# Which engine waits for the last stores: SyncE or GpSimd

## The chip, the cores and the metric

The kernel runs on one core of a Trainium2 chip. The core has five engines that run their own instruction streams and meet only through semaphores: TensorE (PE, matrix products; its weight loads are listed as PEld), VectorE (DVE), ScalarE (ACT), GpSimd (POOL) and SyncE (SP, which here issues transfers and waits). A transfer (DMA) is issued by SyncE or ScalarE and carried out by sixteen DMA engines; when it has landed, its semaphore has been raised by 16.

The metric is the device time of one execution in microseconds. Timed runs give a median; one more execution is recorded by the hardware profiler, and its instructions, waits and transfers can be asked for. An engine's name with a q behind it (SPq) means its instruction queue: waits and the issuing of transfers are listed there.

## The reference

For 2048 rows `x` of width 512 (all in bf16) the kernel computes a gated sum of two branches:

```python
g = sigmoid((x * gate_w).sum(-1, keepdims=True))
# A: 32 heads of width 16
q, k, v = x @ wqkv
phi(t) = concat(softmax(t @ w_phi), softmax(-(t @ w_phi)))   # per head
o = phi(q) @ (phi(k).T @ v) / (phi(q) @ phi(k).sum(rows) + 1e-6)
a = o @ wo
# B
b = relu(x @ w1) @ w2                                        # inner width 1376
out = g * a + (1 - g) * b
```

## The kernel before, in words

The rows are cut into 16 tiles of 128 (numbered m = 0 to 15) and 4 chunks of 512. All of a tile's work is a list of named tasks; each task has an engine, a function that emits its instructions, and the tasks that it depends on. Per chunk: hidden products `h`, the ReLU into `HT`. Per tile or pair of tiles: key and query projections with `w_phi` folded in, softmax features (ScalarE `ex`, VectorE `mx`, `mn`, `sm`, `rc`, GpSimd `t1`, `t2`, `ra`, `nm`), the sum over rows `kv`. Then per tile: a transposing transfer of the query features (`tq`, SyncE), `nd` (numerator and denominator on TensorE, line 654), `rd` and `o` (VectorE, lines 661 and 663), a second transposing transfer `to` (SyncE, line 668), `b` and `a` (TensorE, lines 676 and 682, accumulating both branches in one PSUM bank), the scaled eviction `oe` (line 730 on ScalarE for tiles 0 to 13, line 733 on VectorE for tile 14), and the store `st` to the output (line 735; ScalarE issues it for tiles 0 to 13, SyncE for tile 14).

The last tile is split by columns into 416 and 96: `b15_0`, `a15_0`, `b15_1`, `a15_1` on TensorE (lines 698 and 709), `oe15_0` on ScalarE (line 716), `oe15_1` on VectorE (line 719), and the stores `st15_0`, issued by ScalarE, and `st15_1`, issued by SyncE (both line 722).

The order of the tasks on each engine is written out by hand in the table `ORDER`; nothing is scheduled when the program is built. `_Graph.number` gives each task a semaphore and a count (each transfer its own semaphore, which reaches 16). `settle` works out which waits each task needs, leaving out those already implied by what its engine knows. `emit` writes the waits and instructions, engine by engine (a task's extra waits appear under line 178).

After all engines have been emitted, one more step follows: `unsettled(e, order)` lists the transfers that engine `e` neither waited for nor can infer to have landed, and drops those that another one of the list implies. The engine then waits for each:

```python
        for t in g.unsettled("sp", order):
            nc.sync.wait_ge(sems[t.sem], t.count)
```

For SyncE that list holds six stores, `st11`, `st12`, `st13`, `st14`, `st15_0` and `st15_1`. In the built program they are three instructions on line 751 that wait for two semaphores each: `st14` and `st13`, `st15_0` and `st12`, `st15_1` and `st11`. They are the last instructions of SyncE. The last GpSimd task is `nm_q8` (line 627), the last ones of ScalarE are `oe15_0` and `st15_0`, of VectorE `oe15_1`, of TensorE `a15_1`. No engine but SyncE waits for these last stores.

Of the kernel before, what the change touches and what calls it, by code (L numbers as in the profile page):

```python
# [182 lines left out]
def bass_gated_mix__linear_kernel_hedgehog__dense_activation_relu__prompt_kernel(  # L183
# [38 lines left out]
    with ExitStack() as es:  # L222
# [52 lines left out]
        g = _Graph()  # L275
# [464 lines left out]
        order = g.schedule()  # L740
        g.number(order)
        g.settle(order)
        sems = {e: nc.alloc_semaphore(f"s_{e}") for e in ENGINES}
# [3 lines left out]
        for e, q in (("sp", nc.sync), ("pool", nc.gpsimd), ("act", nc.scalar), ("dve", nc.vector), ("pe", nc.tensor)):  # L747
            g.emit(e, q, order, sems)

        for t in g.unsettled("sp", order):  # L750
            nc.sync.wait_ge(sems[t.sem], t.count)


# [26 lines left out]
```

## Time and profile before

| | |
|---|---|
| timed runs | 149.95, 150.12, 150.76 us; median 150.12 |
| the profiled execution's own time | 149.87 us |
| its span, from the first to the last of the kernel's instructions | 148.3 us |
| TensorE busy | 145.5 us (98%), 1009 matmuls |
| VectorE busy | 111.7 us (75%) |
| GpSimd busy | 109.6 us (74%) |
| ScalarE busy | 91.4 us (62%) |
| granted TensorE clock | 1.000 |
| `out_dram<-OSB` from issue to landing, SyncE: 128 KB, 24 KB | 1.7 us, 1.5 us |
| `out_dram<-OSB` from issue to landing, ScalarE: 128 KB (median of 14), 104 KB | 2.2 us, 1.7 us |

The span covers the kernel's own instructions; the execution's own time is longer, since it takes in what runs around them. Waits, register and branch instructions and the issuing of transfers aren't counted as busy. In the timeline each line gives the start in us from the span's start, the duration in us, the engine, the source line, the operation, what it writes and reads, its shapes and how many were merged; in brackets stands the idle time before it and what ended it. In the view of one source line, three durations (shortest, median, longest, in ns) are followed by the starts of the first and the last instruction. In the view of waits a line gives who waited for whom, the total in us, how often, and the longest.

The trace also keeps a list of every change of a semaphore's value with its time, to the nanosecond, including semaphores that the kernel does not use.

### The profile page before, as it was taken

Reading aid. Unit: us, or ns where it says so; the run is one execution under the profiler, and the core shown is the slowest. Engines: PE = TensorE matmul, PEld = TensorE weight load, DVE = VectorE, ACT = ScalarE, POOL = GpSimd, SP = SyncE. Lnnn points to the kernel's source line nnn. Section 1 sums busy time; section 2 is a strip of 40 time slices with the busy share of each in tenths; the row PEclk is TensorE's granted clock in tenths of the full one; section 3 lists DMA queues with packets and bytes.
Section 4 is the critical chain, followed back from the end, with each engine's and each line's share of the span. In section 5 each row is a group of like instructions: output and inputs, shape, how many; then the busy total and the mean of one; then the engine's idle time right before and its main releaser. Section 6 shows DMA issues by size and latency. Waiting matters only on the chain.

```text
span 148.3 us, 2542 instructions
## 1 busy us (share of the span) xinstructions
PE 145.5 (98%) x1009; PEld 75.3 (51%) x1009; DVE 111.7 (75%) x169; ACT 91.4 (62%) x126; POOL 109.6 (74%) x72
## 2 busy tenths in 40 slices
PE   7999999999999999999999999999999999999994
PEld 2875444445654475445444545455444444445453
DVE  2433666998896948989999997999999988634502
ACT  3475769799969765898983937175583751310141
POOL 4000499999999999999999999999999793150000
PEclk9999999999999999999999999999999999999999
DMA  4998999910040001000000093646957785556752
GB/s 139 324 256 220 169 187 214 340 51 4 0 73 0 0 4 38 0 0 4 0 0 0 7 141 71 141 95 138 183 119 167 180 214 116 141 134 158 64 157 92
DMA packets 46363, 16.11 MB, mean 109 GB/s; under 512 B 39856, under 2 KB 46352, under 8 KB 46352
## 3 DMA queue, kind: packets, MB, share of 16 engines
q1 hardware_dynamic: 43760, 13.61, 42.6%
q10 hardware_dynamic: 2592, 2.34, 4.9%
q8 instruction: 8, 0.13, 0.4%
q14 instruction: 3, 0.02, 0.1%
HBM read 4.41 MB, written 2.10 MB: 44 GB/s over the span
## 4 chain that ended last, share of the span: by engine, by line
PE 98%; DVE 0%; issue 0%
PE PS L676 24%; PE PS L425 21%; PE PS L545 19%; PE PS L526 9%; PE PS L682 9%; PE PS L611 3%; PE PS L654 3%; PE PS L433 2%; PE PS L292 2%; PE PS L698 2%; PE PS L439 2%; PE PS L445 1%; PE PS L408 1%; PE PS L384 1%; PE PS L709 1%; DVE OSB L719 0%
## 5 line engine op out<-in xcount | busy, mean ns | idle before, releaser
L590 POOL TENSOR_TENSOR TS<-PB,MX 128x1024 bf16<-128x1024 bf16 (+1 forms) x18 | 30.9, 1723 | 14.5 <-DVE MX L581 14.5
L676 PE MATMUL PS<-W,HT 128*128 128x512 bf16 (+1 forms) x165 | 38.1, 379 | 0.0
L597 DVE TENSOR_REDUCE ZB<-FT 128x128 f32<-128x2048 bf16 (+1 forms) x18 | 36.6, 2031 | 1.8 <-ACT FT L595 1.8
L595 ACT ACTIVATE FT<-TS 128x2048 bf16<-128x2048 bf16 (+1 forms) x18 | 30.9, 1718 | 9.6 <-POOL TS L590 9.5
L425 PE MATMUL PS<-XT,W 128*128 128x512 bf16 x144 | 34.7, 379 | 0.0
L590 POOL TENSOR_TENSOR TS<-MN,PB 128x1024 bf16<-128x1024 bf16 (+1 forms) x18 | 30.9, 1726 | 0.8 <-DVE MN L583 0.8
L545 PE MATMUL PS<-WP,XT 128*128 128x512 bf16 x128 | 30.6, 379 | 0.0
L604 POOL TENSOR_TENSOR FT<-FT,SC 128x2048 bf16<-128x2048 bf16 (+1 forms) x9 | 29.6, 3293 | 0.0
L503 ACT ACTIVATE HT<-PS 128x512 bf16<-128x512 f32 x40 | 22.6, 597 | 5.4 <-PE PS L425 4.6
L581 DVE TENSOR_REDUCE MX<-PB 128x64 bf16<-128x1024 bf16 (+1 forms) x18 | 19.5, 1085 | 5.9 <-ACT PB L577 5.9
L676 PEld LDWEIGHTS PS<-W,HT 128*128 128x128 bf16 (+1 forms) x165 | 15.4, 98 | 16.9
L730 ACT ACTIVATE OSB<-PS,OMG 128x512 bf16<-128x512 f32 x14 | 9.6, 686 | 21.1 <-PE PS L682 20.5
L583 DVE TENSOR_REDUCE MN<-PB 128x64 bf16<-128x1024 bf16 (+1 forms) x18 | 19.3, 1084 | 3.2 <-ACT PB L577 3.2
L425 PEld LDWEIGHTS PS<-XT,W 128*128 128x128 bf16 x144 | 13.7, 98 | 15.4
L577 ACT ACTIVATE PB<-PS 128x1024 bf16<-128x1024 f32 (+1 forms) x18 | 16.7, 927 | 7.2 <-PE PS L545 4.0
L545 PEld LDWEIGHTS PS<-WP,XT 128*128 128x128 bf16 x128 | 12.1, 98 | 13.5
L526 PE MATMUL PS<-WV,XT 128*128 128x512 bf16 x64 | 16.4, 379 | 0.0
L627 POOL TENSOR_TENSOR FT<-FT,SR 128x1024 bf16<-128x1024 bf16 (+1 forms) x9 | 15.7, 1740 | 0.7
L682 PE MATMUL PS<-WO,OT 128*128 128x512 bf16 x60 | 14.9, 378 | 0.0
L663 DVE SCALAR_TENSOR_TENSOR OTM<-PS,EG,RD 128x256 bf16<-128x256 f32 x32 | 13.8, 463 | 0.2
L661 DVE RECIPROCAL RD<-PS 128x16 f32<-128x16 f32 x32 | 6.4, 232 | 9.0 <-PE PS L654 8.8
L535 ACT ACTIVATE VS<-PS 128x512 bf16<-128x512 f32 x16 | 9.6, 602 | 4.3 <-PE PS L526 4.3
(55 smaller groups left out, 106.6 us busy)
## 6 DMA issues: line engine op xcount, KB each, us to landing
out_dram<-OSB ACTq DMA_DIRECT2D x14, 128.0 KB, 2.2
W<-in_B_w_dram SPq DMA_DIRECT2D x1, 1280.0 KB, 7.5
W<-in_B_w_dram SPq DMA_DIRECT2D x1, 512.0 KB, 4.5
WV<-in_A_wqkv_dram SPq DMA_DIRECT2D x1, 512.0 KB, 4.9
WO<-in_A_wo_dram SPq DMA_DIRECT2D x1, 512.0 KB, 7.5
FT<-in_A_x_dram SPq DMA_DIRECT2D x3, 128.0 KB, 3.1
W<-in_B_w_dram SPq DMA_DIRECT2D x1, 352.0 KB, 4.1
W<-in_B_w_dram ACTq DMA_DIRECT2D x2, 128.0 KB, 3.3
```

Source lines behind the costliest of these rows:

```text
L425: last = q.matmul(PS[:, b, :], W1[:, j, k * P:(k + 1) * P], XT[:, j, chunk(c)], start=(j == 0), stop=(j == ND - 1))
L503: add(f"rl{a}_{k}", "act", lambda q, a=a, k=k, b=b: q.activation(HT[:, k, chunk(a)], PS[:, b, :], ACT.Relu), (prev,), dur=0.6, boost=RL)
L526: last = q.matmul(PS[:, 2, :], XT[:, j, m * P:(m + 1) * P], WV[:, j, :], start=(j == 0), stop=(j == ND - 1))
L545: last = q.matmul(PS[:, n, :], XT[:, j, m * P:(m + 1) * P], WP[:, s, j, :], start=(j == 0), stop=(j == ND - 1))
L581: add(f"mx_{J}", "dve", lambda q, sl=sl, w=w, i=pbg: q.tensor_reduce(MX[:, sl, 0:w * H], i, AX.X, ALU.max), (f"ev_{J}", old("t1")), dur=0. ...
L583: add(f"mn_{J}", "dve", lambda q, sl=sl, w=w, i=pbg: q.tensor_reduce(MN[:, sl, 0:w * H], i, AX.X, ALU.min), (f"ev_{J}", old("t2")), dur=0. ...
L590: add(f"{tn}_{J}", "pool", lambda q, o3=o3, a3=a3, b3=b3: q.tensor_tensor(o3, a3, b3, ALU.subtract), (f"{'mx' if sg == 0 else 'mn'}_{J}", ...
L595: add(f"ex_{J}", "act", lambda q, fs=fs, ts=ts, w=w: q.activation(FT[:, fs, 0:w * F], TS[:, ts, 0:w * F], ACT.Exp), (f"t1_{J}", f"t2_{J}", ...
L597: add(f"sm_{J}", "dve", lambda q, fs=fs, sl=sl, w=w: q.tensor_reduce(ZB[:, sl, 0:2 * w * H], FT[:, fs, 0:w * F].rearrange("p (g d) -> p g ...
L604: add(f"nm_{J}", "pool", lambda q, f3=f3, sl=sl, w=w: q.tensor_tensor(f3, f3, SC[:, sl, 0:2 * w * H].unsqueeze(2).to_broadcast([P, 2 * w * ...
L676: last = q.matmul(PS[:, ab, :], HT[0:r, k, m * P:(m + 1) * P], W2[0:r, k, :], start=(k == 0), stop=False)
L682: last = q.matmul(PS[:, ab, :], OT[:, m % NOT, t, :], WO[:, t, :], start=False, stop=(t == ND - 1))
```

## The change

The engine that is asked what is still unsettled, and that waits for it, is GpSimd instead of SyncE. The list that `unsettled` gives for it holds the same six stores, and the built program the same three instructions, now at the end of GpSimd's stream behind `nm_q8`. SyncE's stream ends with the issue of `st15_1`. Nothing else in the program is different: the streams of TensorE, VectorE and ScalarE are the same, and every transfer stays on its queue.

```diff
-        for t in g.unsettled("sp", order):
-            nc.sync.wait_ge(sems[t.sem], t.count)
+        for t in g.unsettled("pool", order):
+            nc.gpsimd.wait_ge(sems[t.sem], t.count)
```

## The prediction

> **What bounds the kernel now.** I read the chain that ended last first, because it says which engine the whole time belongs to.
>
> ```profile
> ## 4 chain that ended last, share of the span: by engine, by line
> PE 98%; DVE 0%; issue 0%
> ```
>
> TensorE is the bound of the body: 145.5 us busy of 148.3. The change touches no TensorE instruction and nothing ahead of the last stores, so only the end can move. The timeline of the last microseconds shows it, with the issues of the last three stores:
>
> ```profile
> 146.03 0.33 PE L709 MATMUL PS<-WO,OT 128*128 128x96 bf16 x4
> 146.40 0.34 ACTq L722 DMA_DIRECT2D out_dram<-OSB  x1
> 146.40 0.32 DVE L719 TENSOR_SCALAR OSB<-PS,OMG 128x96 bf16<-128x96 f32 x1 [0.59 <-PE PS L709]
> 146.75 0.35 SPq L722 DMA_DIRECT2D out_dram<-OSB  x1
> ```
>
> SyncE's last issue ends at 147.10; the span ends at 148.33. What fills the rest is seen under line 751, first in its own view and then in SyncE's view of waits:
>
> ```profile
> L751 SPq EVENT_SEMAPHORE  x3: 28/28/28, 147.6 to 148.3; - x3
> ```
>
> ```profile
> SPq L751 <- DMA out_dram<-OSB: 1.0, 2, 0.5
> ```
>
> Three waits of 28 ns each end the program, and each begins when a store lands. To the ns, in the trace's list of semaphore changes (which the printed views sum up): st14 has landed at 147.545 and the first wait begins at 147.561; st15_0 at 148.109, the second at 148.125; st15_1 at 148.288, the third at 148.305, and it ends at 148.333, which is the end of the span. So the last landing sets the end, and SyncE follows it by 17 + 28 ns.
>
> The execution's own time is 149.87, that is 1.54 more than the span. The same list shows what lies there: a semaphore, number 2, that no instruction of the kernel touches. It changes five times as engines finish, and four times more:
>
> | round | changes of semaphore 2, us |
> |---|---|
> | before the program | -2.698, -2.654, -2.631, then -2.518, -2.479, -2.445, -2.395 |
> | after it | 146.537, 147.000, 147.038, 147.082, 148.446, then 148.490, 148.529, 148.563, 148.611 |
> | last | 149.399, 149.433, 149.471, 149.515, 149.539, then 149.637, 149.675, 149.710, 149.756 |
>
> (The round before the program has two more changes ahead of those shown, -8.519 and -3.799.) I read this as a relay up through five engines and down again. 146.537 follows TensorE's last matmul by 0.18, 147.000 follows ScalarE's last issue (146.734) by 0.27, and 148.446 follows SyncE's last wait by 0.113. The third and fourth come 38 and 44 ns behind the second, as from engines that had already been waiting: these are GpSimd and VectorE. So SyncE is fifth, the turning point, and four steps of 44, 39, 34 and 48 ns bring the word back to the first. From 148.575 to 149.175 semaphores are cleared, and the last round ends at 149.756. All of that hangs on the step at 148.611.
>
> **The change part by part.**
>
> *Removed from SyncE:* three waits of 28 ns. No instruction is queued behind them, and SyncE's part in the relay comes after the others in either case. Ending at 147.10 instead of 148.33 therefore gains nothing by itself.
>
> *Added to GpSimd:* the same three waits, on the same six stores (st14 with st13, st15_0 with st12, st15_1 with st11). The built program shows the other three engines unchanged and every store still on its queue. GpSimd's last work is long over:
>
> ```profile
> 130.42 0.25 POOL L623 TENSOR_TENSOR SR<-ZB,SC 128x32 f32<-128x32 f32 x1
> 130.75 1.06 POOL L627 TENSOR_TENSOR FT<-FT,SR 128x512 bf16<-128x512 bf16 x1
> ```
>
> It is free at 131.81 and would stand in the first wait for 15.7 us with nothing queued behind it, so it delays no transfer. The first two waits end before the last store lands and are hidden by it; if they were not, each would cost its 28 ns. Only the third is on the path.
>
> *Wake of that wait.* Nothing in the trace shows GpSimd waiting for a store, but it does wait for ScalarE's semaphore twice, in line 178:
>
> ```profile
> L178 POOLq EVENT_SEMAPHORE  x2: 17/17/17, 38.9 to 67.1; - x2
> L178 SPq EVENT_SEMAPHORE  x1: 17/17/17, 140.5 to 140.5; - x1
> ```
>
> The instruction has the same length on both engines. Its start follows the semaphore's change by 25 and 24 ns on GpSimd (38.826 to 38.851, 67.072 to 67.096), against 17 on SyncE: **+8 ns**. An upper bound is the 68 ns from VectorE's semaphore to a GpSimd tensor operation (129.008 to 129.076), that is +51; no gain over 17 can be had, as a wait can't begin before the landing.
>
> The Trainium skill, GPSIMD Engine Reference, section Instruction dispatch, says that a GpSimd operation is passed to eight cores and dispatched there in software, which speaks against using that engine. The two rows of line 178 show a bare wait without such a cost; by that rule the wake would be +51 and the time 0.04 later than I say.
>
> *GpSimd's own ending*, from the end of its last wait to its change of semaphore 2, is not shown, since it fell somewhere in the 15.2 us between 131.81 and 147.038. The nearest rows are SyncE's 0.113, TensorE's 0.18 and ScalarE's 0.27. I take SyncE's, because there too the last instruction is a bare wait with nothing left in the engine: **0**. The ends are -0.06 (an ending no longer than one step, about 0.05) and +0.15 (ScalarE's).
>
> *The relay.* If GpSimd is third, its word must go up two more steps before it comes down. The round before the program shows a late third place: after the gap that ends at -2.698, the steps are 44, 23, 113, 39, 34 and 50, together 303 ns to the last change. From SyncE it was 148.611 - 148.446 = 165. The difference is **+138 ns**. The fourth engine's step down takes 113 instead of 44 because it has only just sent its own word up. If GpSimd is fourth, the sum is 23 + 113 + 39 + 34 + 50 = 259, or +94.
>
> The Trainium skill, Runtime: NRT & Kernel Launch, section The ~15µs preamble/postamble breakdown, describes such a relay over five engines with 44 ns a step. By that figure the two extra steps would be an estimated 88 ns; the trace's late third place measures 138, and the measurement decides.
>
> **Sum:** 8 + 0 + 138 = 146 ns, say +0.15, bounds +0.04 (8 - 60 + 94) and +0.34 (51 + 150 + 138). On the profiled execution that is 149.87 + 0.15 = 150.02. The three timed runs (149.95, 150.12, 150.76) have a median 0.25 above it, so I put the median of the changed kernel at 150.12 + 0.15 = **150.27**. That is 0.1%; a measurement of this kernel can tell about 0.5% (0.75 us) from no change.
>
> **The rivals.**
>
> 1. *GpSimd's ending is long and loses its cover.* This is the case on the slow side. Its place is between the last wait and GpSimd's change of semaphore 2, and today up to 15.2 us of it would be hidden. For it: in the round before the program the third change comes 1.10 behind the second (-3.799 to -2.698), so that engine's part outside the kernel's code can be longer than its neighbours'. Against it: between the two rounds behind the program, the third change (149.471) follows the second by 38 ns, so clearing its semaphores made it no later. If the ending costs 1.10 more than SyncE's, the median is 150.12 + 0.15 + 1.10 = 151.37. It decides from 0.60 on, where the sum passes 0.75.
> 2. *The end gets shorter.* All that lies between the last landing and TensorE's release is 148.611 - 148.288 = 0.32, and a part must stay in any case. Were all of it gone, the median would be 149.80, 0.2% faster: still within 0.5%. Nothing in the profile lets the stores themselves land sooner, as their issues and queues stay.
> 3. *GpSimd doesn't really wait for the last stores.* Then the end would be SyncE's last issue, 147.10, instead of 148.33: 1.23 sooner, a median of 148.89. Against it: all six semaphores stand in the program's last GpSimd instructions.
> 4. *The relay doesn't depend on who is last.* Then only the 8 ns stay and the median is 150.13; no measurement of the whole tells this from the forecast, but the list of semaphore 2 does.
>
> **How the numbers follow.** Forecast (+0.04 to +0.34): 0.78. Rival 4: 0.08. Rival 2: 0.04. Rival 1 at over 0.60: 0.09. Rival 3: 0.01. The forecast, rivals 4 and 2 are all within 0.5%, together 0.90; I move 0.01 of that to each side, because the three runs before lie 0.8 us apart, which gives faster 0.02, same 0.88, slower 0.10. The range goes from the profiled execution with the smallest cost (149.87 + 0.04 = 149.91) to the slowest of the three runs with the forecast's (150.76 + 0.15 = 150.91): 149.9 to 150.9. Most of rival 1 and rival 3 are left outside it.
>
> **What would show it.** In the changed profile, three 28 ns waits of line 751 on GpSimd, the last beginning about 25 ns behind the last landing; a span within 0.05 of 148.3; the first four or five steps of semaphore 2 in a new pattern: two changes at about 147.0 or before, then a gap to about 0.14 past the landing, then 44, 24, about 113, 39, 34, 48. The time outside the span grows from 1.54 to about 1.68. I am wrong if the gap between GpSimd's last wait and its change of semaphore 2 is well over 0.11, if the steps behind it don't add up to about 0.30, or if anything ahead of 146 us differs.

## The result and the profile after

The changed kernel takes 150.82 us (median of 19 runs, 150.00 to 151.31), the kernel before 150.13 (19 runs, 149.85 to 150.76). The ratio is **1.0037, 95% interval 1.0024 to 1.0050**: slower by 0.56 us (0.36 to 0.75). The two medians alone lie 0.69 apart; single runs of one kernel scatter by more than that, so I go by the ratio and its interval. The measured median is inside the range, and the difference is within 0.5% and has the sign that was forecast, but it is nearly four times the 0.15 us of the sum, and its interval leaves out even the sum's upper bound of 0.34. Three executions of the experiments below, one of the first (310.6 us) and two of the kernel in which TensorE waits (257.2 and 542.9), count as slow and are left out of all ratios.

The profiled execution took 151.17, its span is 149.1. The line of the page that gives the chain's shares by engine looks as if something new had come in:

```profile
PE 94%; DMA 3%; SPq 1%; issue 0%; DVE 0%
```

This is the start of the program, not the change. The timeline of TensorE in the changed kernel's first microseconds:

```profile
4.39 1.67 PE L439 MATMUL PS<-XT,W 128*128 128x128 bf16 x12
6.37 0.60 PE L439 MATMUL PS<-XT,W 128*128 128x256 bf16 x4 [0.30 <-DMA W<-in_B_w_dram]
```

TensorE waits here for a first weight chunk, which landed at 6.23; in the profiled execution of before it landed at 4.83. The 33rd matmul starts 0.74 later than before's 33rd, and so does the last, the 1009th: from there on the two bodies run alike, 139.80 us from the 33rd to the last in both. Such a delay comes and goes from run to run: in the ten profiled executions of this document the 33rd matmul starts at 5.87 to 7.09. Over their timed runs the spans of the changed kernel are 147.9 to 149.2, those of the kernel before (35 runs of the first experiments' chip) 147.8 to 149.0. So of the 0.77 us between the two profiled spans (148.333 and 149.101) 0.74 are chance, and the change must be read behind the last landing.

There the changed kernel's timeline has the same last issues, and its view of line 751 the three waits on GpSimd:

```profile
147.13 0.34 ACTq L722 DMA_DIRECT2D out_dram<-OSB  x1
147.14 0.32 DVE L719 TENSOR_SCALAR OSB<-PS,OMG 128x96 bf16<-128x96 f32 x1 [0.59 <-PE PS L709]
147.48 0.35 SPq L722 DMA_DIRECT2D out_dram<-OSB  x1
```

```profile
L751 POOLq EVENT_SEMAPHORE  x3: 43/43/43, 148.3 to 149.1; - x3
```

GpSimd's own last work, in its timeline, ended at 132.55, so it stood there for 16 us:

```profile
131.49 1.06 POOL L627 TENSOR_TENSOR FT<-FT,SR 128x512 bf16<-128x512 bf16 x1
```

The list of semaphore changes tells the rest, to the ns. I call the way from the last landing to the ninth change of semaphore 2 (the last step of the relay) **the end leg**:

| | before (SyncE) | after (GpSimd) | difference |
|---|---|---|---|
| last landing, st15_1 | 148.288 | 149.034 | |
| the last wait begins, behind it | 17 ns | 24 ns | +7 |
| length of the wait | 28 | 43 | +15 |
| ending: from the wait's end to that engine's change of semaphore 2 | 113 | **527** | **+414** |
| steps from there to the ninth change | 44, 39, 34, 48 = 165 | 44, 23, 97, 40, 34, 46 = 284 | +119 |
| end leg | 323 ns | 878 ns | **+555** |

The end leg's 0.555 us is the 0.56 of the timed runs. What lies outside the span says the same without any trace: a run's time less its span is 1.53 (median of the same 35 runs, 1.50 to 1.60) with SyncE, and 2.07 (19 runs, 2.01 to 2.14) with GpSimd.

On one point the prediction read the list wrongly: the clearing of semaphores does not hang on the ninth change as a whole. Its first changes come ahead of that one, at 148.575 against 148.611 before and at 149.828 against 149.912 after. The last round does follow the ninth change at the same distance in both: its first change comes 0.788 us behind.

### The profile page after: what moved, and what is told of

It reads as the page before. It is cut to its first block, busy times and chain, and to the rows that moved or that the text cites. A ratio compares the mean times of both kernels' runs of the same rounds, so it can differ in the third digit from the quotient of the medians.

```text
span 149.1 us, 2542 instructions
## 1 busy us (share of the span) xinstructions
PE 146.0 (98%) x1009; PEld 75.2 (50%) x1009; DVE 111.7 (75%) x169; ACT 91.3 (61%) x126; POOL 109.5 (73%) x72
## 4 chain that ended last, share of the span: by engine, by line
PE 94%; DMA 3%; SPq 1%; issue 0%; DVE 0%
PE PS L676 24%; PE PS L425 21%; PE PS L545 19%; PE PS L526 9%; PE PS L682 9%; DMA W<-in_B_w_dram 3%; PE PS L611 3%; PE PS L654 3%; PE PS L433 2%; PE PS L698 2%; PE PS L445 1%; PE PS L408 1%; PE PS L439 1%; PE PS L709 1%; SPq L306 1%; PE PS L384 0%
```

## The experiments

Theory: GpSimd has an ending of its own of 0.53 us, always, which is exposed when GpSimd ends last, and its place in the relay adds 0.12. Rivals: its standing in a wait slows the body; the cost belongs to the wait for the last landing; the ending is long only because GpSimd has idled for 16 us; it is a drain.

**GpSimd waits early, beside SyncE.** Behind the loop of before:

```diff
+        for n in ("st14", "st13"):
+            nc.gpsimd.wait_ge(sems[n], 16)
```

> SyncE keeps its six waits; GpSimd also waits, but only for st14 and st13. If the cost is GpSimd's own ending (0.53 us from its last wait to its change of semaphore 2) and is exposed only when GpSimd ends last: its change comes 0.59 us after st14's landing, ahead of SyncE's, and the leg from the last landing to the ninth change of semaphore 2 stays at 0.32; ratio 1.000, time 150.1. If GpSimd's standing in a wait for 16 us slows the body (rival): ratio 1.004, time 150.7, with the leg at 0.32.

Ratio 1.0009 (0.9988 to 1.0029), time less span 1.54, end leg 323 ns: the numbers of before. GpSimd's change of semaphore 2 comes at 147.673, 534 ns behind the end of its wait, and SyncE's at 148.014. The long ending is there, and hidden. Standing in the wait costs nothing that shows: TensorE takes 139.80 us from its 33rd matmul to the last here as well.

**GpSimd waits for all but the last landing.**

```diff
+        for n in ("st14", "st13", "st15_0", "st12"):
+            nc.gpsimd.wait_ge(sems[n], 16)
```

> SyncE keeps its six waits; GpSimd waits for st12 to st14 and st15_0, not for the last landing. Fixed ending: GpSimd's change comes about 0.02 + 0.04 + 0.53 = 0.59 us after st15_0's landing, which is some 0.2 ahead of the last one, and 0.28 of relay follows: leg about 0.68, that is +0.36, ratio 1.0024, time 150.5. Rival, body slowed: leg 0.32, ratio 1.004. Rival, the cost belongs to the wait for the last landing itself: leg 0.32, ratio 1.000.

Ratio 1.0030 (1.0013 to 1.0047), time less span 2.01, end leg 775 ns. SyncE still waits for the last landing (its wait ends at 148.028), yet the relay stands until GpSimd's change at 148.478, 528 ns behind the end of its own last wait. This refutes a price of the last landing, and the leg alone accounts for the ratio (0.45 us, 0.3%), which leaves nothing for a slowed body. (TensorE takes 0.19 longer here from its 33rd matmul to the last, 139.99, but that arises within the first 21.3 us, long before GpSimd begins to wait.) The leg is 0.09 over the expected one, because the wait for st15_0 was the first of two here and the second followed it:

```profile
L753 POOLq EVENT_SEMAPHORE  x2: 43/43/43, 147.8 to 147.9; - x2
```

The two start 86 ns apart, at 147.821 and 147.907.

**The other engines as the waiting one.** In each, both names of the loop are replaced:

```diff
-        for t in g.unsettled("sp", order):
-            nc.sync.wait_ge(sems[t.sem], t.count)
+        for t in g.unsettled("act", order):
+            nc.scalar.wait_ge(sems[t.sem], t.count)
```

and likewise with `"dve"` and `nc.vector`, `"pe"` and `nc.tensor`.

> ScalarE waits instead of SyncE. If each engine has an ending of its own and ScalarE's is the 0.27 us seen behind its last issue, and it is second in the relay (38 + 44 + 23 + 98 + 39 + 34 + 47 = 323 ns): leg 0.02 + 0.03 + 0.27 + 0.32 = 0.64, +0.32, ratio 1.002, time 150.45. If an ending behind a bare wait is 0.11 on every engine but GpSimd: leg 0.48, ratio 1.001.

> VectorE waits instead of SyncE. It should be fourth: the steps behind its change are 23 + 98 + 39 + 34 + 47 = 241 ns. With an ending like SyncE's on a slower sequencer (0.14): leg 0.02 + 0.04 + 0.14 + 0.24 = 0.44, +0.12, ratio 1.001. With an ending like GpSimd's (0.53): leg 0.83, +0.51, ratio 1.0034.

> TensorE waits instead of SyncE. It is first in the relay, so all eight steps follow: 34 + 38 + 44 + 23 + 98 + 39 + 34 + 47 = 357 ns. With the ending of 0.18 us seen behind its last matmul and a wait of about 0.08: leg 0.04 + 0.08 + 0.18 + 0.36 = 0.66, +0.34, ratio 1.002.

The views of line 751 of the three kernels, in this order:

```profile
L751 ACTq EVENT_SEMAPHORE  x3: 38/38/38, 147.8 to 148.6; - x3
```

```profile
L751 DVEq EVENT_SEMAPHORE  x3: 49/49/50, 147.2 to 148.0; - x3
```

```profile
L751 PEldq EVENT_SEMAPHORE  x3: 51/51/51, 148.1 to 148.9; - x3
```

The first two waits end ahead of the last landing in each (the second by 0.11 to 0.13 us), so one wait stands on the path. With the list of semaphore changes (ns; the last two columns are of the timed runs, the time less the span in us):

| waits last | begins | wait | ending | steps behind | end leg | ratio | less span |
|---|---|---|---|---|---|---|---|
| SyncE (before) | 17 | 28 | 113 | 165 | 323 | 1 | 1.53 |
| ScalarE | 21 | 38 | 110 | 324 | 493 | 1.0020 (1.0003 to 1.0037) | 1.67 |
| VectorE | 27 | 50 | 140 | 241 | 458 | 1.0005 (0.9983 to 1.0027) | 1.44 |
| TensorE | 28 | 51 | 187 | 357 | 623 | 1.0026 (1.0004 to 1.0048) | 1.80 |
| GpSimd (the change) | 24 | 43 | 527 | 284 | 878 | 1.0037 (1.0024 to 1.0050) | 2.07 |

The steps behind grow in the order SyncE, VectorE, GpSimd, ScalarE, TensorE, which fixes the relay's order upward as TensorE, ScalarE, GpSimd, VectorE, SyncE. Behind a bare wait four engines end in 0.11 to 0.19 us; GpSimd alone takes 0.53. For ScalarE the first of the two expectations had 0.27, the way from the end of an issue; behind a wait it is 0.11, as the second had it. Of these three, TensorE and ScalarE are slower by an interval that leaves out 1; the VectorE kernel can't be told from before.

**GpSimd kept busy until shortly before.** Ahead of the changed loop:

```diff
+        fs = nc.alloc_semaphore("fil")
+        for n in range(48):
+            if n:
+                nc.gpsimd.wait_ge(fs, n)
+            nc.gpsimd.iota(FIL[:, :], [[1, P]], channel_multiplier=0).then_inc(fs, 1)
```

> As the changed kernel, but GpSimd first runs 48 small iotas into a tile of its own (extra work, nothing else reads it), so that it is busy for about 15 us behind its last task and stands in the first wait for under 1 us. Fixed ending: 0.53 us from its last wait to its change of semaphore 2, leg 0.88, ratio 1.004. Rival, the ending is long because GpSimd has been idle for 16 us: ending 0.11 to 0.27, leg 0.46 to 0.62, ratio 1.001 to 1.002.

The view of that line shows the extra work, from the end of GpSimd's last task on:

```profile
L755 POOL IOTA FIL<- x48: 234/234/237, 131.8 to 146.1; 128x128 int32 x48
```

The last iota ends at 146.31 and the first wait begins at 147.66, so GpSimd stands for 1.35 us there (under 1 was expected) instead of 16. The ending is 527 ns, the end leg 880, the ratio 1.0044 (1.0027 to 1.0062). The long idling has no part in it.

**A memset behind the waits.** Behind the changed loop:

```diff
+        nc.gpsimd.memset(FIL[:, :], 1.0)
```

> As the changed kernel, with one 128x1 memset (about 0.1 us) on GpSimd behind the waits (extra work, nothing reads it). Fixed ending counted from the last instruction: 0.53 behind the memset, leg about 0.88 + 0.15 = 1.03, ratio 1.005. Rival, most of the ending wakes an idle engine, which the memset then does: 0.53 counted from the last wait, leg about 0.88, ratio 1.004.

```profile
L753 POOL MEMSET FIL<- x1: 102/102/102, 148.7 to 148.7; 128x1 bf16 x1
```

508 ns lie between the memset's end (148.777) and GpSimd's change (149.285); the end leg is 1031 ns, ratio 1.0053 (1.0034 to 1.0073). The ending is counted from the last instruction, here the memset, and follows directly on work: the rival, that it wakes an idle engine, falls.

**Two drains behind the waits.**

```diff
+        for _ in range(2):
+            nc.gpsimd.drain()
```

> As the changed kernel, with two drain instructions on GpSimd behind the waits (extra work). GpSimd's ending is 0.41 us longer than SyncE's. If that is a drain of GpSimd at the end of the program: each of the two takes about 0.4 us, leg about 1.7, ratio 1.009; or, if only the first drain has something to do, one takes about 0.4 and the ending behind it is near 0.11, leg about 0.9. Rival, an idle GpSimd drains at once: each takes under 0.06 us (as one at the start of the program ended 0.05 behind the last memset), the ending stays at 0.53, leg about 0.95, ratio 1.0045.

The view of that line:

```profile
L753 POOLq DRAIN  x2: 34/40/46, 148.9 to 149.0; - x2
```

46 and 34 ns, and an ending of 524 behind them; the end leg is 1027 (0.95 us was expected: from the end of the last wait to that of the second drain 150 ns pass). An idle GpSimd drains at once, so a drain of this kind isn't the missing 0.41 us. The ratio, 1.0073 (1.0053 to 1.0093; four runs), is above the 1.0047 that the leg explains; the spans of these few runs lie high (median 149.05 against 148.5). Of that, 0.17 are the wait and the drains themselves, which end 218 ns behind the last landing instead of 45; the rest fits a late load at the start, which is seen in the profiled execution (the 33rd matmul starts at 6.84 instead of 6.36) and not shown for the other three.

Taking the ending or the relay away isn't possible from the kernel, since neither is made of its instructions. What fills GpSimd's 0.53 us stays open: the trace lists no instruction there. It was 508 to 534 ns in all six profiled kernels in which GpSimd's last instruction stands late enough for its ending to be read. No kernel of these is faster than the one before by an interval that leaves out 1.

## Why the prediction was right or wrong

- **Only the end moves, and nothing is queued behind the waits: right.** The first experiment shows it directly, and the body of 139.80 us is the same with either engine waiting. A span within 0.05 of 148.3 was not seen, and was a bad sign to name: spans of one kernel scatter by over 1 us through the first loads.
- **SyncE's earlier end gains nothing: right**, as its change now simply follows VectorE's by 23 ns.
- **Wake, +8 ns: right**, 24 ns behind the landing against 17. The length was not the same, though: the rows of line 178 (17 ns on both engines) are waits for one semaphore, and these wait for two, which take 28 ns on SyncE and 43 on GpSimd. The rule of the Trainium skill that I weighed here (GPSIMD Engine Reference, Instruction dispatch) adds nothing to a bare wait: by it the wake would have been 68 ns behind the landing.
- **GpSimd's own ending, taken as SyncE's, at most 0.15 over it: wrong, and the step that failed.** It measured 527 ns, 414 over SyncE's, which is the prediction's own first sign of being wrong. I reasoned that a bare wait leaves nothing in the engine; four engines end within 0.19 us behind one, and this one does not. The trace of before left room for 15 us; I closed it with rows of other engines, which bound nothing about this one.
- **The relay, +138 ns: right in kind, measured +119.** GpSimd is third; the turn at VectorE took 97 ns instead of 113. I had taken the steps from the round before the program. The last round behind it, in the same table, has that turn as 98 ns (149.539 to 149.637), and its steps from the third change on (44, 24, 98, 38, 35, 46) would have given 285 - 165 = +120. Rival 4 (no dependence on who is last) falls with the table. By the 44 ns a step that the Trainium skill gives (Runtime: NRT & Kernel Launch, The ~15µs preamble/postamble breakdown) the estimate was 88; measured in the changed kernel, the single steps are 23 to 46 and the turn 97.
- **Rival 1, a long ending that loses its cover: the mechanism is what happened**, at 0.41 us instead of the 1.10 that I priced and under the 0.60 from which I let it decide. The time outside the span grew to 2.07, not 1.68. So the likeliest outcome (within 0.5%) and the range held, with the rival's mechanism as the larger part of the sum. That the median lies in the range is luck: the sum's own bounds, 0.04 to 0.34, missed the 0.56, and the range reached up to 150.9 only because the slowest of three runs before was taken for its upper end.
- **Rivals 2 and 3 did not occur:** the end got longer, and GpSimd's last wait began 24 ns behind the last landing.

## What to carry to other kernels

An engine that finishes long before the end may hide work outside the kernel's own instructions; ending the program on it exposes that work, and its busy rows say nothing of the size. Here SyncE is the best tried place for the last waits but for VectorE, whose time can't be told from it although its end leg is 0.135 longer, and GpSimd the worst: 0.56 us for moving three waits that take 0.1 in all. When the difference sought is below the scatter of whole times, measure from the last event that both kernels share (here the last landing), not from the start.

## What the runs showed of the hardware that was not expected

- A wait for two semaphores takes 28 ns on SyncE, 38 on ScalarE, 43 on GpSimd, 50 on VectorE and 51 on TensorE. A wait for one takes 17 on SyncE, ScalarE and GpSimd, 21 on VectorE and 51 on TensorE, where the second semaphore thus adds nothing.
- In the first experiment the built wait names the two semaphores the other way round, st13 ahead of st14, and the profile shows one GpSimd wait of 2258 ns: it begins 23 ns behind the landing of st13, the one named first (144.858), and ends 29 behind that of st14 (147.110), so most of the time of standing is shown as its length. In all the other waits for two, the store named first landed last, or both had landed.

```profile
L753 POOLq EVENT_SEMAPHORE  x1: 2258/2258/2258, 144.9 to 144.9; - x1
```

- In nine of the ten profiled executions the device time runs 0.10 to 0.11 us longer than from the span's start to the last listed change of semaphore 2. In the VectorE kernel it is 0.12 shorter than that (149.47 against 149.592), and its time less span is 1.44 in the timed runs too (1.38 to 1.47). So what closes the device time is not that change alone; which event it is stays open.
